# Transposed attention scores in exact widths and three banks per head, in a windowed-attention and SwiGLU-gate kernel

## The chip, the cores and the metric

One core of one Trainium2 chip. The metric is the device time of one execution in microseconds, the median over several runs. All inputs and outputs are float32 in HBM.

## The reference

```python
x = A_x                                   # 1 x 2048 x 512
xn = layernorm(x)
# A: attention, 32 heads of 16, query i sees keys i-255 .. i
q, k, v = split(xn @ wqkv)                # wqkv 512 x 1536
p = softmax(where(mask, q @ k.T * 16 ** -0.5, -1e9))
s = (p @ v) @ wo                          # wo 512 x 512
# B: SwiGLU, F = 1792
b = (silu(xn @ w_gate) * (xn @ w_up)) @ w_down
out = x + s * silu(b)
```

## The kernel before

**Stages.** The 2048 tokens go in four chunks of 512. For each chunk the kernel normalises and transposes x, projects q and k (`Proj`, tile a), v (`Values`, vp), the two halves of the SwiGLU (`GateUp`, g and u), its down projection (`Down`, d) and the output projection (`Wo`, s). All of these are "dense" matmuls of float32 values that are split into a high and a low part (format fp32r) and multiplied in three combinations. Their weights are fetched once per chunk (wr), split by ScalarE into wh (line 425) and by GpSimd into wl (line 428).

**Two streams on TensorE.** Each matmul uses 64 of the 128 rows of the array. Row group 0 does one half of each contraction, row group 1 the other, and both run side by side; `next_mm(r)` emits the next matmul of stream r. Short jobs of the attention are put in `extra[r]` and go first.

**Attention.** A unit u is one chunk and four heads; there are 32 units, 8 for each chunk. For each unit:

- b (`max_pair`, line 946): scores of 128 queries against up to 384 keys; VectorE takes the masked row maximum (line 954). The matmul is at least 256 columns wide: `w = max(n, 256)`.
- mt (`max_turn`, line 980): transposes the maxima, which are then put as an extra row into q by a small DMA, negated.
- c (`prob_pair`, line 1097): transposed scores, keys on the partitions and queries on the columns, minus the maximum. `pieces(c, e)` says which key blocks kb go into bank e of a head: each entry is (kb, first query block, columns of the matmul, place in the bank, first and last column that are used). ScalarE takes the exponential of the used columns (line 1058) and writes it into a round buffer p of `PCAP` columns (`p_place`, `p_take`); GpSimd sets the blocks on the two edges of the window to zero (`masks`, lines 1071 and 1075).
- pv (`pv_visit`, line 1134): the value product of the whole unit in plain fp32, 32 output columns for each head; after it the unit's part of p is free.

PSUM has 8 banks: four (`pf`) for the dense tiles and four (`pr`, `rb_free`) that b, c, mt, xp (the transposes of later chunks) and pv share.

**Order.** The program is written out by a planner while it is built: it keeps clocks of its own for TensorE's two streams (`issue(r, cols)`: `cols * 0.000444 + 0.004` us for a matmul) and for VectorE, ScalarE and GpSimd (`do(engine, ready, cost, ...)`), and issues what is due and ready by these clocks. `plan_attention` gives the due times: in `streams[1]` the score pairs of unit u from u + 1.07 on, its value product at u + 1.89, where 1 is the dense work of a unit (`PACE` = 17.6 us). Each engine then runs its instructions in this order.

Of the kernel before, what the change touches and what calls it, by code (L numbers as in the profile page):

```python
# [35 lines left out]
NEG = -1.0e30  # L36
QUART = ((0, 4), (4, 7), (7, 11), (11, 14))
NHID = 8
PCAP = 6784
NSL = 12  # L40
SPARE = 3
LAG = 7
# [13 lines left out]
def tile_window_attention_swiglu_gate(  # L56
# [305 lines left out]
    def half(r):  # L362
        return slice(R * r, R * r + R)
# [568 lines left out]
    def max_pair(u, p, qb):  # L932
        c = u // NG
        lo = qb * P
        n = 3 * P
        if c == 0 and qb < 2:
            lo, n = HALO, (qb + 1) * P
        w = max(n, 256)
        m = mts[u % 2]
        for h in range(2):  # L940
            j = 2 * p + h
            r = R * h
            pb, tag = bank(rb_free, f"b{u}_{qb}_{j}")

            def go(pb=pb, r=r):
                nc.tensor.matmul(  # L946
                    pb[:, :w], qs[u % 3][r : r + 48, p, qb * P : (qb + 1) * P],
                    ks[u % 3][r : r + 48, p, lo : lo + w], start=True, stop=True,
                )

            def ttr(pb=pb, j=j):
                junk = sb(f"jk{u}_{qb}_{j}", [P, 3 * P], BF16, "jk", 1)
                col = 8 * (j % 2) + 4 * (j // 2) + qb
                nc.vector.tensor_tensor_reduce(  # L954
                    junk[:, :n], pb[:, :n], maskb[:, 3 * P - n :], 1.0, -3.0e38,
                    ALU.add, ALU.max, m[:, col : col + 1],
                )

            def after(t, tag=tag):
                rb_free[tag] = t  # L960
                ttr_at[u] = ttr_at.get(u, []) + [t]

            extra[h].append((w, go, lambda t, ttr=ttr, after=after: do("V", t, 0.23 + 0.00098 * n, ttr, after, 0.0)))

    mtp = {}

# [40 lines left out]

    def pieces(c, e):
        if c == 0:
            return ([(3, 2, 256, 0, 128, 256), (2, 2, 256, 256, 256, 512)],  # L1010
                    [(0, 0, 384, 0, 0, 384)], [(1, 1, 384, 0, 0, 384)])[e]
        return ([(3, 2, 256, 0, 128, 256), (-2, 0, 256, 256, 256, 384)],
                [(-1, 0, 256, 0, 0, 256), (2, 2, 256, 256, 256, 512)],
                [(0, 0, 384, 0, 0, 384)], [(1, 1, 384, 0, 0, 384)])[e]

    pt = {}
    pt_at = {}
# [16 lines left out]
        p_next[0] = at + h * n  # L1034
        return pbuf[:, at : at + h * n].rearrange("p (h n) -> p h n", h=h)

    def prob_span(u, e):
        pcs = pieces(u // NG, e)
        return min(q[4] for q in pcs), max(q[5] for q in pcs)

    def prob_ready(u, e, p):
        a, b = prob_span(u, e)
        if p_place(2 * (b - a)) is None:
            return None
        return latest([ms_at.get(u), bank_time(rb_free, 2), p_freed[0]])

# [2 lines left out]
    def prob_pair(u, e, p):  # L1049
        c = u // NG  # L1050
        pcs = pieces(c, e)
        a, b = prob_span(u, e)
        t = p_take(2, b - a, u)
        pt[u, e, p] = t, a
        left = [2]

        def exp(h, pc):
            nc.scalar.activation(t[:, h, :], pc[:, a:b], AF.Exp, scale=DH ** -0.5)  # L1058

        blocks = []  # L1060
        for kb, qb, w, at0, v0, v1 in pcs:
            q0 = qb + (v0 - at0) // P
            for blk in range((v1 - v0) // P):
                if q0 + blk == kb or q0 + blk == kb + 2:
                    blocks.append((v0 + blk * P, q0 + blk == kb))

        def masks():
            for at, diagonal in blocks:
                s = t[:, :, at - a : at - a + P]
                if diagonal:  # L1070
                    nc.gpsimd.affine_select(  # L1071
                        s, s, [[0, 2], [1, P]], ALU.is_ge, 0.0, base=0, channel_multiplier=-1
                    )
                else:
                    nc.gpsimd.affine_select(  # L1075
                        s, s, [[0, 2], [-1, P]], ALU.is_gt, 0.0, base=0, channel_multiplier=1
                    )

        def after(tm, tag):
            rb_free[tag] = tm  # L1080
            left[0] -= 1
            if left[0] == 0:
                if blocks:
                    do("G", tm, 0.36 * len(blocks), masks, lambda t: pt_at.__setitem__((u, e, p), t), 0.0)
                else:
                    pt_at[u, e, p] = tm

        for h in range(2):
            r = R * h
            pc, tag = bank(rb_free, f"c{u}_{e}_{2 * p + h}")  # L1090

            def finished(t, h=h, pc=pc, tag=tag):
                do("S", t, 0.06 + 0.00081 * (b - a), lambda: exp(h, pc), lambda t: after(t, tag), 0.0)

            for i, (kb, qb, w, at0, _, _) in enumerate(pcs):
                def go(i=i, k0=HALO + kb * P, qb=qb, w=w, at0=at0, r=r, pc=pc):
                    nc.tensor.matmul(  # L1097
                        pc[:, at0 : at0 + w], ks[u % 3][r : r + 49, p, k0 : k0 + P],
                        qs[u % 3][r : r + 49, p, qb * P : qb * P + w],
                        start=(i == 0), stop=True, skip_group_check=True,  # L1100
                    )

                extra[h].append((w, go, finished if i == len(pcs) - 1 else None))
# [10 lines left out]
    def pv_visit(u, es):  # L1114
        c, g = divmod(u, NG)
        pbs = [bank(rb_free, f"pv{u}_{r}") for r in range(2)]
        jobs = [[], []]
        for e in es:
            for kb, qb, w, at0, v0, v1 in pieces(c, e):
                for r in range(2):  # L1120
                    k64 = 2 * kb + r
                    a, b = max(k64, 0), min(k64 + 5, 8)
                    jobs[r].append((b - a, e, kb, R * a, R * b, at0 + R * a - P * qb))
        for r in range(2):
            jobs[r].sort(key=lambda o: -o[0])
        begun = set()
        cost = 0.3
        for both in zip(*jobs):
            for r in range(2):
                n, e, kb, q0, q1, at = both[r]  # L1130
                assert vheld[(4 * c + kb) % VT, g // 4] == 4 * c + kb
                for j in range(4):
                    t, a = pt[u, e, j // 2]
                    nc.tensor.matmul(  # L1134
                        pbs[r][0][32 * j : 32 * j + 32, q0:q1],
                        vt[half(r), (4 * c + kb) % VT, VW * (4 * g + j) : VW * (4 * g + j) + 32],
                        t[half(r), j % 2, at - a : at - a + q1 - q0],
                        start=(r, j) not in begun, stop=True, skip_group_check=True,
                    )
# [41 lines left out]
    def plan_attention():  # L1181
        for u in range(NU):
            c = u // NG
            if u:
                marks.append((u - 1 + 0.3, load_qk, (u,)))
            for n in range(8):
                streams[0].append((u + 0.02 + 0.1 * n, max_ready, max_pair, (u, n // 4, n % 4)))
            streams[0].append((u + 0.8, turn_ready, max_turn, (u, 0)))
            streams[0].append((u + 0.8, turn_ready, max_turn, (u, 1)))
            ne = 3 if c == 0 else 4  # L1190
            for n in range(2 * ne):
                streams[1].append((u + 1.07 + 0.1 * n, prob_ready, prob_pair, (u, n // 2, n % 2)))
            streams[1].append((u + 1.89, pv_ready, pv_visit, (u, tuple(range(ne)))))
        for c in range(1, NCH):
            marks.append((8 * c - 4.9, load_x, (c,)))
# [261 lines left out]
```

## Time and profile before

| | |
|---|---|
| median of 3 runs | 871.28 us |
| lowest, highest | 868.6, 871.69 us |
| span of the profiled execution | 871.9 us |
| that execution's own time | not given beside its span |
| TensorE matmuls, weight loads | 864.0 us, 796.8 us busy, 11976 each |
| VectorE, ScalarE, GpSimd | 501.9, 486.7, 624.7 us busy |
| DMA | 139.63 MB |

How to read the profile: PE is TensorE's matmuls, PEld its weight loads, DVE VectorE, ACT ScalarE, POOL GpSimd, SP the engine that issues DMAs. A group's row gives the line of the kernel, the engine, the operation, output and inputs by the program's names, the shapes, the count, then busy us and the mean ns of one, and the idle time before them with what ended it. A matmul's record is longer than the time that it holds its stream, since matmuls are pipelined: the pace is read from start to start. In rows of the timeline the first two numbers are start and length in us. In rows of a window they are the window, its length, then busy us and count for PE, PEld, DVE, ACT and POOL, the granted share of TensorE's clock, the DMA share and GB/s. The launch parameters of the program are in the last lines of the kernel.

### The profile page before, as it was taken

Reading aid. Unit: us, or ns where it says so; the run is one execution under the profiler, and the core shown is the slowest. Engines: PE = TensorE matmul, PEld = TensorE weight load, DVE = VectorE, ACT = ScalarE, POOL = GpSimd, SP = SyncE. Lnnn points to the kernel's source line nnn. Section 1 sums busy time; section 2 is a strip of 40 time slices with the busy share of each in tenths; the row PEclk is TensorE's granted clock in tenths of the full one; section 3 lists DMA queues with packets and bytes.
Section 4 is the critical chain, followed back from the end, with each engine's and each line's share of the span. In section 5 each row is a group of like instructions: output and inputs, shape, how many; then the busy total and the mean of one; then the engine's idle time right before and its main releaser. Section 6 shows DMA issues by size and latency. Waiting matters only on the chain.

```text
span 871.9 us, 30169 instructions
## 1 busy us (share of the span) xinstructions
PE 864.0 (99%) x11976; PEld 796.8 (91%) x11976; DVE 501.9 (58%) x1663; ACT 486.7 (56%) x1040; POOL 624.7 (72%) x900
## 2 busy tenths in 40 slices
PE   9999999999999999999999999999999999999997
PEld 8799989898999998999999989999899989999897
DVE  4264476654765566666566676566655765554234
ACT  3345555555666465655576556665656665566431
POOL 4466587668777777867697797677768778869771
PEclk9999999999999999999999999999999999999999
DMA  5675846566686974766677877556667778654442
GB/s 138 157 182 126 235 115 173 125 161 166 149 200 181 261 190 103 145 159 133 151 181 193 220 178 200 120 147 144 169 141 187 160 194 208 163 132 112 104 124 79
DMA packets 69489, 139.63 MB, mean 160 GB/s; under 512 B 14546, under 2 KB 23250, under 8 KB 69348
## 3 DMA queue, kind: packets, MB, share of 16 engines
q1 hardware_dynamic: 69060, 137.18, 63.4%
q8 instruction: 94, 1.54, 0.8%
q10 hardware_dynamic: 288, 0.52, 0.2%
q14 instruction: 47, 0.39, 0.2%
HBM read 107.74 MB, written 29.62 MB: 158 GB/s over the span
## 4 chain that ended last, share of the span: by engine, by line
PE 96%; DMA 1%; DVE 1%; issue 1%; SPq 0%; ACT 0%; POOL 0%; DVEq 0%; ACTq 0%
PE u L457 19%; PE d L457 18%; PE g L457 17%; PE a L457 11%; PE pv L1134 8%; PE c L1097 5%; PE s L457 5%; PE b L946 5%; PE vp L457 5%; PE warm L234 1%; DMA den<-od 1%; DVE jk L954 0%; SPq L95 0%; PE xp L475 0%; POOL wl L428 0%
## 5 line engine op out<-in xcount | busy, mean ns | idle before, releaser
L428 POOL TENSOR_TENSOR wl<-wr,wh 128x512 fp32r<-128x512 f32 (+3 forms) x258 | 307.6, 1211 | 84.8 <-ACT wh L425 82.2
L954 DVE CUSTOM_DVE_ANT_0 jk<-b,maskb 128x384 bf16<-128x384 f32 (+2 forms) x512 | 271.3, 530 | 125.2 <-PE b L946 62.8
L1058 ACT ACTIVATE p<-c 128x384 f32<-128x384 f32 (+1 forms) x480 | 209.1, 489 | 129.6 <-PE c L1097 107.2
L457 PE MATMUL d<-wh,hh 64*128 64x256 f32 x1792 | 258.7, 278 | 0.3 <-DVE ho L454 0.3
L457 PEld LDWEIGHTS d<-wh,hh 64*128 64x128 f32 x1792 | 224.4, 185 | 1.5 <-issue 0.6
L457 PE MATMUL d<-wl,hh 64*128 64x256 f32 x896 | 203.5, 277 | 0.0
L425 ACT ACTIVATE wh<-wr 128x512 fp32r<-128x512 f32 (+3 forms) x258 | 142.1, 593 | 50.0 <-PE a L457 10.6
L457 PE MATMUL g<-xh,wh 64*128 64x512 f32 x448 | 169.0, 397 | 0.0
L457 PE MATMUL u<-xl,wh 64*128 64x512 f32 x448 | 168.3, 395 | 0.0
L457 PE MATMUL u<-xh,wh 64*128 64x512 f32 x448 | 168.3, 395 | 0.0
L457 PE MATMUL u<-xh,wl 64*128 64x512 f32 x448 | 167.9, 395 | 0.0
L457 PE MATMUL g<-xl,wh 64*128 64x512 f32 x448 | 167.0, 395 | 0.0
L457 PE MATMUL g<-xh,wl 64*128 64x512 f32 x448 | 166.7, 395 | 0.0
L1071 POOL TENSOR_SCALAR_AFFINE_SELECT p<-p 128x256 f32<-128x256 f32 x256 | 104.7, 414 | 78.8 <-ACT p L1058 75.6
L457 PEld LDWEIGHTS d<-wl,hh 64*128 64x128 f32 x896 | 147.6, 185 | 0.2
L946 PE MATMUL b<-k,q 48*128 48x384 f32 (+1 forms) x512 | 119.7, 335 | 0.5 <-DVE m L954 0.4
L1097 PE MATMUL c<-q,k 49*128 49x384 f32 (+1 forms) x704 | 115.3, 303 | 0.3 <-DVE m L954 0.3
L1075 POOL TENSOR_SCALAR_AFFINE_SELECT p<-p 128x256 f32<-128x256 f32 x224 | 92.5, 414 | 15.9 <-ACT p L1058 14.3
L457 PE MATMUL a<-xh,wh 64*128 64x512 f32 x256 | 99.1, 401 | 0.1
L457 PE MATMUL a<-xl,wh 64*128 64x512 f32 x256 | 98.5, 400 | 0.1
L601 POOL TENSOR_TENSOR hh<-h,hh 128x512 fp32r<-128x512 f32 x56 | 72.7, 1298 | 36.1 <-ACT hh L597 35.8
L457 PE MATMUL a<-xh,wl 64*128 64x512 f32 x256 | 98.3, 399 | 0.0
(114 smaller groups left out, 2096.7 us busy)
## 6 DMA issues: line engine op xcount, KB each, us to landing
wr<-wgu SPq DMA_DIRECT2D x112, 256.0 KB
k<-qkd SPq DMA_DIRECT2D x48, 192.0 KB
wr<-wqk SPq DMA_DIRECT2D x32, 256.0 KB
qkd<-qkh SPq DMA_DIRECT2D x32, 256.0 KB
qkd<-qkl SPq DMA_DIRECT2D x32, 256.0 KB
q<-qkd SPq DMA_DIRECT2D x64, 128.0 KB
wr<-wdn SPq DMA_DIRECT2D x32, 256.0 KB
od<-ev SPq DMA_DIRECT2D x32, 256.0 KB
```

The source lines that it names most:

```text
L234: nc.tensor.matmul(wbank[:, : rhs.shape[-1]], warm, rhs, start=True, stop=True)
L425: nc.scalar.activation(hi[0][pr, a:b], raw[pr, a:b], AF.Copy)
L428: nc.gpsimd.tensor_tensor(lo[0][pr, a:b], raw[pr, a:b], f32(hi[0][pr, a:b]), op=ALU.subtract)
L457: return nc.tensor.matmul(pb, a, b, start=first, stop=last, skip_group_check=True)
L601: nc.gpsimd.tensor_tensor(hl[:, 1, :], self.h, f32(hl[:, 0, :]), op=ALU.subtract)
L946: nc.tensor.matmul(pb[:, :w], qs[u % 3][r : r + 48, p, qb * P : (qb + 1) * P], ks[u % 3][r : r + 48, p, lo : lo + w], start=True, stop=True,)
L954: nc.vector.tensor_tensor_reduce(junk[:, :n], pb[:, :n], maskb[:, 3 * P - n :], 1.0, -3.0e38, ALU.add, ALU.max, m[:, col : col + 1],)
L1058: nc.scalar.activation(t[:, h, :], pc[:, a:b], AF.Exp, scale=DH ** -0.5)
L1071: nc.gpsimd.affine_select(s, s, [[0, 2], [1, P]], ALU.is_ge, 0.0, base=0, channel_multiplier=-1)
L1075: nc.gpsimd.affine_select(s, s, [[0, 2], [-1, P]], ALU.is_gt, 0.0, base=0, channel_multiplier=1)
L1097: nc.tensor.matmul(pc[:, at0 : at0 + w], ks[u % 3][r : r + 49, p, k0 : k0 + P], qs[u % 3][r : r + 49, p, qb * P : qb * P + w], start=(i == ...
L1134: nc.tensor.matmul(pbs[r][0][32 * j : 32 * j + 32, q0:q1], vt[half(r), (4 * c + kb) % VT, VW * (4 * g + j) : VW * (4 * g + j) + 32], t[hal ...
```

## The change

The matmuls of the scores get the width that is used: line 946 uses n columns, and `pieces` gives widths 128, 256 and 384 that fill three banks of 512 columns per head in chunks 1 to 3 (before: four banks with 256, 512, 384 and 384 used columns), and three banks with 512, 384 and 256 columns in chunk 0 (before 384 each). The exponential then covers a whole bank. The round buffer p grows from 6784 to 8192 columns, and a launch parameter sets the scratch for dynamic DMAs to 1024. The planner's price of an exponential and the due times of the score pairs are set anew.

```diff
-PCAP = 6784
+PCAP = 8192
...
-        w = max(n, 256)
...
-                    pb[:, :w], qs[u % 3][r : r + 48, p, qb * P : (qb + 1) * P],
-                    ks[u % 3][r : r + 48, p, lo : lo + w], start=True, stop=True,
+                    pb[:, :n], qs[u % 3][r : r + 48, p, qb * P : (qb + 1) * P],
+                    ks[u % 3][r : r + 48, p, lo : lo + n], start=True, stop=True,
...
-            extra[h].append((w, go, lambda t, ttr=ttr, after=after: do("V", t, 0.23 + 0.00098 * n, ttr, after, 0.0)))
+            extra[h].append((n, go, lambda t, ttr=ttr, after=after: do("V", t, 0.23 + 0.00098 * n, ttr, after, 0.0)))
...
     def pieces(c, e):
         if c == 0:
-            return ([(3, 2, 256, 0, 128, 256), (2, 2, 256, 256, 256, 512)],
-                    [(0, 0, 384, 0, 0, 384)], [(1, 1, 384, 0, 0, 384)])[e]
-        return ([(3, 2, 256, 0, 128, 256), (-2, 0, 256, 256, 256, 384)],
-                [(-1, 0, 256, 0, 0, 256), (2, 2, 256, 256, 256, 512)],
-                [(0, 0, 384, 0, 0, 384)], [(1, 1, 384, 0, 0, 384)])[e]
+            return ([(3, 3, 128, 0), (0, 0, 384, 128)], [(1, 1, 384, 0)], [(2, 2, 256, 0)])[e]
+        return ([(3, 3, 128, 0), (0, 0, 384, 128)], [(-2, 0, 128, 0), (1, 1, 384, 128)],
+                [(-1, 0, 256, 0), (2, 2, 256, 256)])[e]
...
-    def prob_span(u, e):
-        pcs = pieces(u // NG, e)
-        return min(q[4] for q in pcs), max(q[5] for q in pcs)
+    def prob_cols(u, e):
+        return sum(q[2] for q in pieces(u // NG, e))
...
-        if p_place(2 * (b - a)) is None:
+        if p_place(2 * prob_cols(u, e)) is None:
...
-            nc.scalar.activation(t[:, h, :], pc[:, a:b], AF.Exp, scale=DH ** -0.5)
+            nc.scalar.activation(t[:, h, :], pc[:, :n], AF.Exp, scale=DH ** -0.5)
...
-                do("S", t, 0.06 + 0.00081 * (b - a), lambda: exp(h, pc), lambda t: after(t, tag), 0.0)
+                do("S", t, 0.17 + 0.00084 * n, lambda: exp(h, pc), lambda t: after(t, tag), 0.0)
...
-            ne = 3 if c == 0 else 4
+            ne = 3
             for n in range(2 * ne):
-                streams[1].append((u + 1.07 + 0.1 * n, prob_ready, prob_pair, (u, n // 2, n % 2)))
+                streams[1].append((u + 1.07 + 0.13 * n, prob_ready, prob_pair, (u, n // 2, n % 2)))
...
-    nc = bacc.Bacc("TRN2", target_bir_lowering=False, num_devices=1)
+    nc = bacc.Bacc("TRN2", target_bir_lowering=False, num_devices=1, dynamic_dma_scratch_size=1024)
```

More of the change, by code (lines that the diff above doesn't have):

```diff
@@ L1035, in p_take @@
         return pbuf[:, at : at + h * n].rearrange("p (h n) -> p h n", h=h)
-    def prob_span(u, e):
-        pcs = pieces(u // NG, e)
-        return min(q[4] for q in pcs), max(q[5] for q in pcs)
+    def prob_cols(u, e):
+        return sum(q[2] for q in pieces(u // NG, e))
     def prob_ready(u, e, p):
-        a, b = prob_span(u, e)
-        if p_place(2 * (b - a)) is None:
+        if p_place(2 * prob_cols(u, e)) is None:
             return None
@@ L1051, in prob_pair @@
         pcs = pieces(c, e)
-        a, b = prob_span(u, e)
-        t = p_take(2, b - a, u)
-        pt[u, e, p] = t, a
+        n = prob_cols(u, e)
+        t = p_take(2, n, u)
+        pt[u, e, p] = t
         left = [2]
         def exp(h, pc):
-            nc.scalar.activation(t[:, h, :], pc[:, a:b], AF.Exp, scale=DH ** -0.5)
+            nc.scalar.activation(t[:, h, :], pc[:, :n], AF.Exp, scale=DH ** -0.5)
         blocks = []
[L1061 to L1065, printed above, removed]
+        for kb, qb, w, at0 in pcs:
+            for q in range(qb, qb + w // P):
+                if q == kb or q == kb + 2:
+                    blocks.append((at0 + (q - qb) * P, q == kb))
         def masks():
             for at, diagonal in blocks:
-                s = t[:, :, at - a : at - a + P]
+                s = t[:, :, at : at + P]
                 if diagonal:
@@ L1092, in finished @@
             def finished(t, h=h, pc=pc, tag=tag):
-                do("S", t, 0.06 + 0.00081 * (b - a), lambda: exp(h, pc), lambda t: after(t, tag), 0.0)
-            for i, (kb, qb, w, at0, _, _) in enumerate(pcs):
+                do("S", t, 0.17 + 0.00084 * n, lambda: exp(h, pc), lambda t: after(t, tag), 0.0)
+            for i, (kb, qb, w, at0) in enumerate(pcs):
                 def go(i=i, k0=HALO + kb * P, qb=qb, w=w, at0=at0, r=r, pc=pc):
@@ L1118, in pv_visit @@
         for e in es:
-            for kb, qb, w, at0, v0, v1 in pieces(c, e):
+            for kb, qb, w, at0 in pieces(c, e):
                 for r in range(2):
@@ L1132, in pv_visit @@
                 for j in range(4):
-                    t, a = pt[u, e, j // 2]
+                    t = pt[u, e, j // 2]
                     nc.tensor.matmul(
@@ L1136, in pv_visit @@
                         vt[half(r), (4 * c + kb) % VT, VW * (4 * g + j) : VW * (4 * g + j) + 32],
-                        t[half(r), j % 2, at - a : at - a + q1 - q0],
+                        t[half(r), j % 2, at : at + q1 - q0],
                         start=(r, j) not in begun, stop=True, skip_group_check=True,
```

## The prediction

> **What bounds the kernel now.** I read the page first, then the chain of waits, then the waits of the weight loads, then the groups by form, and last the order of time around single matmuls.
>
> ```profile
> span 871.9 us, 30169 instructions
> PE 864.0 (99%) x11976; PEld 796.8 (91%) x11976; DVE 501.9 (58%) x1663; ACT 486.7 (56%) x1040; POOL 624.7 (72%) x900
> ```
>
> TensorE has work in flight for 99% of the span; the other three have slack on average. The chain says the same by line:
>
> ```profile
> by line: PE u L457 19.0%; PE d L457 18.0%; PE g L457 17.2%; PE a L457 11.1%; PE pv L1134 8.3%; PE c L1097 5.5%; PE s L457 5.4%; PE b L946 4.7%; PE vp L457 4.7%; PE warm L234 1.3%; DMA den<-od 1.2%; issue 0.5%; DVE jk L954 0.5%; SPq L95 0.4%
> 836.24 15.43 PE d L457 x265
> ```
>
> The second line gives the pace. Two streams run side by side, one for each half of the array's rows; 265 matmuls of 256 columns take 15.43 us, so one takes 2 x 15.43 / 265 = 0.1165 us in its stream, 0.455 ns for a column. The scores c (L1097) hold 5.5%, 48.0 us, and their columns alone explain it: the rows below count 448 x 256 + 256 x 384 = 212,992 columns, half of them in each stream, and 106,496 x 0.455 ns = 48.5 us. So each score matmul costs its columns, and putting it between the dense ones costs next to nothing.
>
> ```profile
> L1097 PE MATMUL c<-q,k 49*128 49x256 f32 x448 | 57.9, 282 | 0.3 <-DVE m L954 0.3
> L1097 PE MATMUL c<-q,k 49*128 49x384 f32 x256 | 57.4, 340 | 0.0
> L946 PE MATMUL b<-k,q 48*128 48x256 f32 x64 | 13.3, 283 | 0.1
> L457 PE MATMUL g<-xh,wh 64*128 64x512 f32 x448 | 169.0, 397 | 0.0
> PEld pv L1134 <- issue: 4.9, 16, 0.4
> PEld pv L1134 <- POOL p L1075: 1.7, 5, 0.4
> PEld b L946 <- ACT p L1058: 0.4, 2, 0.2
> ```
>
> The last three are waits of the weight loads (total us, times, longest): these are small. Nothing but shorter PE streams can make this kernel much faster.
>
> **The change part by part.**
>
> *Narrower matmuls (the term that decides).* Per head, chunks 1 to 3 go from widths 256, 256, 256, 256, 384, 384 to 128, 384, 128, 384, 256, 256: two of 256 become 128. Chunk 0 goes from 256, 256, 384, 384 to 128, 384, 384, 256: one. Line 946 loses one for each head of chunk 0 (block 0). With 24 units of four heads and 8 of chunk 0 that is 192 + 32 + 32 = 256 matmuls, 128 in each stream. The count stays (704 and 512). By columns alone each would save 128 x 0.455 = 0.058 us, so 128 x 0.058 = 7.4 us at most.
>
> But a matmul needs its own weight load. Around 478 us a 64-column matmul (mt) sits in the stream of g, and shortly after one in that of vp:
>
> ```profile
> 478.19 0.40 PE L457 MATMUL g<-xl,wh 64*128 64x512 f32 x1
> 478.42 0.22 PE L980 MATMUL mt<-ident,m 64*80 64x64 f32 x1
> 478.45 0.47 PE L457 MATMUL g<-xh,wl 64*128 64x512 f32 x1
> 478.77 0.39 PE L457 MATMUL g<-xh,wh 64*128 64x512 f32 x1
> 478.76 0.27 PE L457 MATMUL vp<-wl,xh 64*128 64x256 f32 x1
> 478.89 0.25 PE L980 MATMUL mt<-ident,m 64*80 64x64 f32 x1
> 478.95 0.36 PE L457 MATMUL vp<-wh,xl 64*128 64x256 f32 x1
> 479.15 0.27 PE L457 MATMUL vp<-wh,xh 64*128 64x256 f32 x1
> 478.19 0.11 PEld L980 LDWEIGHTS mt<-ident,m 64*80 64x80 f32 x1
> 478.43 0.19 PEld L457 LDWEIGHTS g<-xh,wl 64*128 64x128 f32 x1
> 478.54 0.19 PEld L457 LDWEIGHTS g<-xh,wh 64*128 64x128 f32 x1
> ```
>
> From the g of 478.19 to that of 478.77 are 0.58 us, which hold two streams of 512 columns (2 x 0.233) and mt: mt took 0.114 us, about what 256 columns take, though it has 64. The loads say why: the load for the g behind mt begins at 478.43, when mt itself starts, and the next one only 0.11 later. The g that started at 478.45 shows 0.47 instead of 0.40: it stood waiting for its weights. In the vp stream mt cost 0.39 - 0.233 = 0.157, with a wait of its own in it. At the head of the kernel the loads stand alone:
>
> ```profile
> 10.65 0.28 PE L234 MATMUL warm<-rs,warm 128*128 128x4 f32 x2
> 10.55 0.30 PEld L234 LDWEIGHTS warm<-rs,warm 128*128 128x128 f32 x2
> 10.76 1.64 PEld L234 LDWEIGHTS warm<-warm 128*128 128x128 f32 x14
> 12.33 1.78 PEld L350 LDWEIGHTS xp<-ident,xt 128*128 128x128 f32 x16
> ```
>
> Two matmuls of 4 columns still take (10.76 - 10.55) / 2 = 0.105 us each, and sixteen of 128 columns (1.78 - 0.14) / 15 = 0.109. So a load of 128 columns has a pace of 0.105 to 0.114 us, and I take 0.109, the row with the width in question. A narrowed matmul then saves 0.1165 - 0.109 = 0.0075 us, 128 of them **1.0 us**. Bounds: at 0.105 it is 1.5 us; at full column pace 7.4 us; at 0.157 a loss of 128 x 0.04 = 5.2 us. The narrow shape itself does not occur in this trace in this number format.
>
> [...]
>
> *Exponentials.* Per head of chunks 1 to 3, before 256, 512, 384 and 384 columns, after three of 512; in chunk 0 384 three times becomes 512, 384, 256.
>
> ```profile
> L1058 ACT ACTIVATE p<-c 128x384 f32<-128x384 f32 x288 | 125.6, 490 | 63.7 <-PE c L1097 44.5 <-PE u L457 7.5 <-PE g L457 3.1
> L1058 ACT ACTIVATE p<-c 128x512 f32<-128x512 f32 x96 | 52.4, 597 | 25.0 <-PE c L1097 23.0 <-PE d L457 1.2 <-POOL wl L428 0.6
> L1058 ACT ACTIVATE p<-c 128x256 f32<-128x256 f32 x96 | 31.3, 381 | 40.9 <-PE c L1097 39.8 <-POOL p L1075 0.9
> L1071 POOL TENSOR_SCALAR_AFFINE_SELECT p<-p 128x256 f32<-128x256 f32 x256 | 104.7, 414 | 78.8 <-ACT p L1058 75.6 <-DMA q<-qkd 1.3 <-DMA k<-qkd 0.9
> L428 POOL TENSOR_TENSOR wl<-wr,wh 128x512 fp32r<-128x512 f32 x214 | 273.9, 1297 | 79.5 <-ACT wh L425 77.9 <-PE a L457 1.5
> ```
>
> That is 0.381 + 0.597 + 2 x 0.490 = 1.958 against 3 x 0.597 = 1.791 us, 0.167 less for each of 96 heads: ACT loses 16 us of 487. It idles 44% of the span and PE waits for it 0.4 us in all (the row above), so 0 is taken and 0.4 is the gain's end. A bank of scores is held longer by one exponential (0.597 instead of 0.490), but two pairs in eight fall away, so bank time falls.
>
> *Masks.* The blocks per unit stay at 8 for each pair of heads (6 in chunk 0). They come as 3, 3, 2 instead of 2, 2, 2, 2. What queues behind a batch on POOL is the split of weights (wl, 1.297 us each) and of hidden tiles, which dense matmuls need; a batch grows by one mask, 0.414 us. The last batch before the value product has two masks before and after, so its lateness stays. I take 0.
>
> *Buffer.* A unit fills 4 x 1536 = 6144 columns of p. Of 6784, 640 remain, room for one pair of 2 x 256 ahead of the value product; of 8192, 2048 remain, for two pairs of 2 x 512. The next unit's first pair is due 0.18 of a unit after that product, so room seldom decides; 0, with the 4.9 us of the row pv <- issue as an end for whatever is gained around the product.
>
> *The launch parameter* for DMA scratch.
>
> ```profile
> wr<-wgu SPq DMA_DIRECT2D x112, 256.0 KB
> ...
> xt<-x ACTq DMA_DIRECT2D x2, 256.0 KB
> ```
>
> These are the first of the 25 groups of DMA issues and the only one that is not SP's; POOL issues none, and no instruction names the parameter: 0. [...]
>
> *The planner.* It orders all instructions by a clock of its own. It will price a narrow matmul at 128 x 0.000444 + 0.004 = 0.061 us instead of the 0.109 I expect, so it believes PE earlier than it is; the other engines then have more time than planned, which does no harm. Its price of an exponential rises from 0.371 (for 384) to 0.600 (for 512), near the rows. The order of everything behind the first score shifts a little. Waits that a new order makes or removes I bound by the waits above, 3 us to either side.
>
> The sum: the median of the runs is 871.28 us, between 868.6 and 871.69; the page has only a span for its execution, 871.9, which is 0.6 above the median. Span 871.9 - 1.0 = 870.9; median 871.3 - 1.0 = **870.3 us**. Part of the runs' 3 us can be the clock at the start:
>
> ```profile
> 20.00:24.00 4.00, 4.00 (x21) 3.10 (x20) 0.15 (x1) 1.15 (x2) 0.63 (x2) 0.50 0.65 170
> L946 PE MATMUL b<-k,q x512: 275/337/443, 44.2 to 787.9; 48*128 48x384 f32 x149, 48*128 48x256 f32 x22
> ```
>
> For these 4 us TensorE had half its clock (0.50), which costs 2 us; the change touches nothing before the first score (b, 44.2 us), so this can fall either way.
>
> **The rivals.**
>
> *Columns count in full.* If the load for the matmul behind a narrow one ran further ahead, each would save 0.058 us: 871.3 - 7.4 = 863.8 us. For it: c's share of the chain matches its columns. Against: that is shown from 256 columns up, where the stream (0.1165) outlasts the load (0.109), and the load at 478.43 starts with mt, not before. [...]
>
> *Slower: a narrow matmul of this format runs like plain fp32.* For it: no matmul of this format under 256 columns is in the trace, so nothing there excludes it. A plain fp32 matmul of 128 columns is two instructions, seven calls in the row warm x14, each record (12.33 - 10.76) / 14 = 0.112, together 0.224 us: 0.108 more than now, 128 x 0.108 = 13.8 us, 885.1 us. It decides if it holds for any width under 256. Against: 282, 340 and 397 ns at 256, 384 and 512 columns lie on a line without a step, and each is one instruction.
>
> *Slower: the bunched masks arrive late.* If each of 24 value products waits for one mask more, 24 x 0.414 = 9.9 us, 881 us; half of that, 876. Against: the last batch does not grow, and five such waits make 1.7 us now.
>
> *A better order.* Fewer pairs and more room ahead of the value product, so that the 4.9 us of pv <- issue vanish with the 1.0: 865.4.
>
> **How the numbers follow.** Load pace 0.55; full columns 0.15; plain fp32 0.11; late masks 0.10; better order 0.09. A measurement of this kernel can tell about 0.5%, 4.4 us, from no change: 866.9 to 875.6. Faster: full columns, half of the better order (what is left of the waits decides) and 0.02 of the first case, 0.22. Slower: plain fp32, most of the late masks, and 0.07 of the first case where a narrow matmul costs as much as mt in the vp stream (871.3 + 5.2), 0.27. Same: 0.51. The range reaches from 863.6, the full columns, to 879, which takes in the 5.2 and most of the late masks; outside it are plain fp32 and the far end of the masks.
>
> **What would show it.** Right: c and b matmuls of 128 columns at about 282 - 58 = 224 ns long, one instruction each, the matmul behind one with a lengthened record as g had (0.47), and loads 0.11 apart; c's share of the chain near 5.4%; 384 exponentials; masks at 480. Wrong upward: two records for a narrow matmul, or one well over 280 ns. Wrong downward: c's share at 4.9% or less, and the matmul behind a narrow one at its usual length. Late masks would show as waits of pv for L1071 or L1075 in tens of times.

## The result and the profile after

The changed kernel takes 875.71 us (median of 6 runs, 873.07 to 878.75), the kernel before 871.12 (6 runs beside it): ratio 1.0055 [1.0033, 1.0077]. It is slower by about 4.6 us. Two further series gave 1.0024 [1.0005, 1.0044] and 1.0050 [1.0031, 1.0068]. The time lies inside the range on record, but the likeliest case was no change that can be told, and the small loss came from a step that had been priced at nothing, with 3 us to either side.

The profiled execution after is the slowest of its six: span 877.0 us, time 878.75. That of before has a span of 871.9, with 6.8 us of half clock at the start (17.7 to 24.6 us) that this one hasn't, which costs it 3.4 us. So the 5.1 us between the spans are not the loss itself.

The page:

```profile
span 877.0 us, 29908 instructions
PE 863.3 (98%) x11976; PEld 798.4 (91%) x11976; DVE 504.4 (58%) x1663; ACT 478.4 (55%) x944; POOL 623.1 (71%) x900
```

TensorE's count is as before, one record for each narrow matmul, ACT has 96 instructions fewer and is busy 8.3 us less. The groups by form (busy us, mean ns of one, idle before and what ended it):

```profile
L1053 ACT ACTIVATE p<-c 128x512 f32<-128x512 f32 x320 | 172.9, 596 | 109.7 <-PE c L1091 105.3 <-PE a L457 1.8 <-PE b L945 1.8
L1065 POOL TENSOR_SCALAR_AFFINE_SELECT p<-p 128x256 f32<-128x256 f32 x256 | 102.4, 413 | 66.6 <-ACT p L1053 59.9 <-DMA wr<-wdn 6.6
L1069 POOL TENSOR_SCALAR_AFFINE_SELECT p<-p 128x256 f32<-128x256 f32 x224 | 91.9, 413 | 22.0 <-ACT p L1053 20.8 <-DMA k<-qkd 0.9
L1091 PE MATMUL c<-q,k 49*128 49x384 f32 x256 | 65.0, 384 | 0.0
L1091 PE MATMUL c<-q,k 49*128 49x128 f32 x224 | 38.6, 226 | 3.0 <-DMA q<-ms 3.0
L1091 PE MATMUL c<-q,k 49*128 49x256 f32 x224 | 30.7, 280 | 0.0
L945 PE MATMUL b<-k,q 48*128 48x128 f32 x32 | 5.9, 229 | 0.7 <-DMA k<-qkd 0.7
```

The narrow matmul has one record of 226 ns (forecast about 224). 256 columns are as long as they were; 384 have 384 ns instead of 340, since many now stand behind a narrow one and wait for their weights (a place at 564 us below shows it; where the experiments widen the 128 again, they have 337 and 342 ns). Masks are 480, exponentials 384. New is the idle time in the fifth row: 3.0 us before the first c of two units, ended by the small DMA q<-ms that puts the maxima into q. The chain of waits (start, us, what) has that DMA twice among its ten longest pieces, at 98.68 and 243.68:

```profile
98.68 6.54 DMA q<-ms
243.68 6.71 DMA q<-ms
```

The timeline shows what it does, first SP's queue, then TensorE, then the windows (the number after POOL's is the granted clock):

```profile
97.22 1.36 SPq L95 DMA_DIRECT2D wr<-wgu  x1
98.68 0.60 SPq L95 DMA_DIRECT2D q<-ms  x1
```

```profile
105.35 0.55 PE L1091 MATMUL c<-q,k 49*128 49x128 f32 x4 [1.69 <-DMA q<-ms]
...
106.57 0.62 PE L457 MATMUL u<-xl,wh 64*128 64x512 f32 x1
```

```profile
20.00:24.00 4.00, 4.00 (x34) 3.19 (x34) 0.15 (x1) 0.28 (x1) 1.30 (x2) 1.00 0.90 221
104.00:106.00 2.00, 0.65 (x9) 0.68 (x11) 0.38 (x2) 0.09 (x1) 0.43 (x1) 1.00 1.09 360
106.00:108.00 2.00, 2.00 (x20) 2.00 (x18) 0.15 (x1) 1.16 (x3) 0.93 (x3) 0.55 1.02 227
108.00:110.00 2.00, 2.00 (x20) 2.00 (x18) 0.77 (x3) 0.92 (x2) 1.21 (x4) 0.59 1.02 173
```

The q<-ms of 8 KB is issued right behind a weight transfer and lands 6.5 us later; the planner takes it as landed 3.5 us after the transfers ahead of it. The c that needs it stands first in TensorE's queue and everything waits 1.69 us. Then the clock is granted at 0.55 and 0.59 for two windows, which loses 2 x 0.45 + 2 x 0.41 = 1.7 us more. In the first row the start runs at full clock.

How far the changed kernel is behind the kernel before, taken at the same dense matmul (the n-th of 7680) of both traces:

| place in the changed kernel (us) | behind (us) | what lies there |
|---|---|---|
| 16.0 | +1.5 | first dense matmul, after a longer wait at the head |
| 35.9 | -1.6 | full clock where before had half |
| 99.3 | -1.5 | |
| 118.5 | +1.8 | wait for q<-ms, then half clock |
| 245.2 | +2.2 | |
| 282.7 | +4.4 | wait of 1.34 for q<-ms at 250, then 0.85 by 283 in no single place |
| 311.5 | +5.4 | wait of 1.38 (issue) at 298 |
| 381.0 | +5.9 | |
| end | +5.1 | |

Behind 400 us the distance wanders, as the orders differ, but it no longer grows: its median is 4.5 to 5.8 us in each 100 us. So nothing is lost at every unit, as late masks or a dear narrow matmul would lose it; the loss sits at a few places.

### The profile page after: what moved, and what is told of

Same layout as the page of the kernel before. It is cut to its first block, busy times and chain, and to the rows that moved or that the text cites. A ratio compares the mean times of both kernels' runs of the same rounds, so it can differ in the third digit from the quotient of the medians.

```text
span 877.0 us, 29908 instructions
## 1 busy us (share of the span) xinstructions
PE 863.3 (98%) x11976; PEld 798.4 (91%) x11976; DVE 504.4 (58%) x1663; ACT 478.4 (55%) x944; POOL 623.1 (71%) x900
## 4 chain that ended last, share of the span: by engine, by line
PE 92%; DMA 4%; POOL 1%; DVE 1%; issue 1%; SPq 1%; ACT 1%; ACTq 0%; POOLq 0%; DVEq 0%
PE d L457 18%; PE u L457 18%; PE g L457 17%; PE a L457 10%; PE pv L1128 8%; PE c L1091 6%; PE s L457 5%; PE vp L457 5%; PE b L945 4%; DMA q<-ms 2%; PE warm L234 1%; DMA wr<-wgu 1%; POOL wl L428 1%; DMA k<-qkd 1%; SPq L95 1%
## 5 line engine op out<-in xcount | busy, mean ns | idle before, releaser
L1053 ACT ACTIVATE p<-c 128x512 f32<-128x512 f32 (+2 forms) x384 | 197.3, 569 | 129.7 <-PE c L1091 121.8
L457 PE MATMUL u<-xl,wh 64*128 64x512 f32 x448 | 164.4, 397 | 0.0
L457 PE MATMUL u<-xh,wh 64*128 64x512 f32 x448 | 164.1, 397 | 0.0
L457 PE MATMUL g<-xh,wh 64*128 64x512 f32 x448 | 163.8, 395 | 0.0
L457 PE MATMUL u<-xh,wl 64*128 64x512 f32 x448 | 163.1, 396 | 0.0
L945 PE MATMUL b<-k,q 48*128 48x384 f32 (+2 forms) x512 | 122.7, 331 | 2.2 <-DMA out<-y 0.8
L1091 PE MATMUL c<-q,k 49*128 49x128 f32 (+2 forms) x704 | 103.4, 300 | 3.0 <-DMA q<-ms 3.0
L457 PE MATMUL a<-xh,wh 64*128 64x512 f32 x256 | 94.3, 394 | 0.1
L457 PE MATMUL a<-xl,wh 64*128 64x512 f32 x256 | 94.0, 394 | 0.1
L1091 PEld LDWEIGHTS c<-q,k 49*128 49x128 f32 x704 | 84.4, 187 | 6.9 <-DVE m L953 2.3
```

Source lines behind the costliest of these rows:

```text
L457: return nc.tensor.matmul(pb, a, b, start=first, stop=last, skip_group_check=True)
L945: nc.tensor.matmul(pb[:, :n], qs[u % 3][r : r + 48, p, qb * P : (qb + 1) * P], ks[u % 3][r : r + 48, p, lo : lo + n], start=True, stop=True,)
L1053: nc.scalar.activation(t[:, h, :], pc[:, :n], AF.Exp, scale=DH ** -0.5)
L1091: nc.tensor.matmul(pc[:, at0 : at0 + w], ks[u % 3][r : r + 49, p, k0 : k0 + P], qs[u % 3][r : r + 49, p, qb * P : qb * P + w], start=(i == ...
```

## The experiments

Two readings stood against each other: the price of the new matmuls, or the order that the planner makes of the same work. Each series has its own runs of the kernel before on the same chip.

**What a narrow matmul costs.** First the changed kernel's order, with the 256 narrow matmuls issued with 256 columns again:

```diff
-                    pb[:, :n], qs[u % 3][r : r + 48, p, qb * P : (qb + 1) * P],
+                    pb[:, : max(n, 256)], qs[u % 3][r : r + 48, p, qb * P : (qb + 1) * P],
...
-            return ([(3, 3, 128, 0), (0, 0, 384, 128)], [(1, 1, 384, 0)], [(2, 2, 256, 0)])[e]
+            return ([(3, 3, 128, 384), (0, 0, 384, 0)], [(1, 1, 384, 0)], [(2, 2, 256, 0)])[e]
...
+                    if w == P:
+                        back = 1 if at0 else 0
+                        qb, w, at0 = qb - back, 2 * P, at0 - back * P
```

> The changed kernel with its order untouched, but all 256 matmuls of 128 columns issued with 256 columns again (the surplus lands in places that the next matmul of the bank overwrites). Theory A (a load of weights sets the pace, 0.110 us, so narrowing saved next to nothing and the loss comes from the new order): 0.6 to 1.5 us slower than the changed kernel, about 876.5. Rival B (columns count in full, and the new order lost some 12 us): 7 us slower, 883. Rival C (a narrow matmul costs more than a wide one, and that is the loss): 3 to 6 us faster, 870 to 873.

And the changed kernel unaltered, beside it:

> The changed kernel itself once more, on the same chip as the others: 875.7 us by every theory, within 2 us; the profile shows whether PE again waits for the small DMA q<-ms near 105 and 250 us (theory A: at least one of the two waits, 1 to 2 us each, since the order puts the first c of the unit 5 us behind that DMA).

Measured: 878.08 us, 1.0072 [1.0046, 1.0098], against 874.08, 1.0024 [1.0005, 1.0044] for the changed kernel. Widening costs 4.0 us [1.3, 6.7]: more than the 1 us that the load pace gives and less than the 7.4 of full columns. But the two profiles differ in waits too, so this pair doesn't give the size. The same pair was taken in an order without the wait (the next experiment's edit and the widening together):

> The kernel of e4 (changed kernel, q<-ms counted as landed 3 us later) with its order untouched, and the 256 narrow matmuls issued with 256 columns again. Here no wait for q<-ms stands in the way of the price. Theory A (load of weights sets the pace): 0.5 to 1.5 us slower than e4, 873.3; behind a narrow c the next matmul comes 0.110 to 0.114 us later in e4, behind a wide one 0.117 to 0.120 here. Rival B (columns count in full): 7 us slower, 879. Rival C (narrow costs more than wide): faster than e4, 869 to 871.

Measured: 873.7 us, 1.0034 [1.0015, 1.0053], where that order with narrow matmuls gave 1.0005 and 1.0017: 2 us, with an uncertainty of about 2. To multiply the cost instead, the 224 score matmuls of 256 columns were issued as two of 128:

```diff
+                    for x in range(0, w, P if w == 2 * P else w):
+                        y = P if w == 2 * P else w
...
-                        pc[:, at0 : at0 + w], ks[u % 3][r : r + 49, p, k0 : k0 + P],
-                        qs[u % 3][r : r + 49, p, qb * P : qb * P + w],
+                            pc[:, at0 + x : at0 + x + y], ks[u % 3][r : r + 49, p, k0 : k0 + P],
+                            qs[u % 3][r : r + 49, p, qb * P + x : qb * P + x + y],
```

> The kernel of e4 with its order untouched, and each of its 224 c matmuls of 256 columns issued as two of 128, with the same weights loaded for each. Columns stay the same, loads grow by 224, 112 in each stream. Theory A (a narrow matmul costs its load, 0.112 us): 112 x (2 x 0.112 - 0.119) = 11.8 us slower than e4, about 884. Rival B (columns count, loads are hidden): within 1 us of e4, 872 to 873.

> The kernel of e4 once more, as the base for e9 on the same chip: 0 to 2 us from the kernel before by every theory; no wait of PE for q<-ms.

Measured: 883.95 us, 1.0144 [1.013, 1.0158], against 872.31, 1.0017 [1.0002, 1.0033]: 11.6 us [10.9, 12.4]. If columns decided, two halves would cost what one whole does. 112 pairs in each stream take 11.64 / 112 = 0.104 us more than one matmul of 256 columns (0.1165), so one narrow matmul takes (0.1165 + 0.104) / 2 = 0.110 us. The groups of the split kernel, loads and matmuls of c:

```profile
L1093 PEld LDWEIGHTS c<-q,k 49*128 49x128 f32 x928 | 96.0, 186 | 3.9 <-DVE m L953 0.9
L1093 PE MATMUL c<-q,k 49*128 49x128 f32 x672 | 76.3, 248 | 0.6 <-DVE m L953 0.6
```

The 224 further loads are there and no wait of any size is new: the time goes into loads. One place in the unsplit kernel shows it singly, TensorE's matmuls and then its loads:

```profile
563.95 0.39 PE L457 MATMUL a<-xl,wh 64*128 64x512 f32 x1
...
564.18 0.22 PE L1091 MATMUL c<-q,k 49*128 49x128 f32 x1
...
564.24 0.40 PE L1091 MATMUL c<-q,k 49*128 49x384 f32 x2
564.47 0.39 PE L457 MATMUL a<-xh,wl 64*128 64x512 f32 x1
```

```profile
564.18 0.19 PEld L1091 LDWEIGHTS c<-q,k 49*128 49x128 f32 x2
564.29 0.19 PEld L457 LDWEIGHTS a<-xh,wl 64*128 64x128 f32 x1
```

Between the two a of one stream, 0.52 us apart, lie 512 columns of a (0.233) and a c of 128 and of 384 columns, which take 0.29 together. Taking 384 x 0.455 = 0.175 off leaves 0.115 for the narrow one. The load of the 384 columns begins as the narrow matmul starts, and that of the next a 0.11 later.

**The wait for q<-ms.** The planner takes the maxima as landed 3 us later than it did:

```diff
-            dma(t, put, lambda t: ms_at.__setitem__(u, t), -3.0, 8)
+            dma(t, put, lambda t: ms_at.__setitem__(u, t + 3.0), -3.0, 8)
```

In the changed kernel:

> The changed kernel with one planner constant more: the small DMA q<-ms counts as landed 3 us later, so the first scores c of a unit are ordered later. Theory A: PE's waits for q<-ms near 105 and 250 us go, 3 to 4 us, 872. Rivals C and D (loss by the narrow matmuls or by three banks): 875 to 876.

In the kernel before:

> The kernel before with the same margin of 3 us for q<-ms in the planner. Theory A (the loss is PE waiting for q<-ms, which the kernel before had only once, 0.4 us): as before, 870.5 to 873. Rival E (the margin helps any version by some 3 us, so e4 is only the changed kernel plus an unrelated gain): 868 to 870.

Measured: changed kernel 872.31, 1.0005 [0.9988, 1.0022], and 1.0017 in the repeat above; kernel before 874.73, 1.0037 [1.0022, 1.0052]. TensorE's waits of the changed kernel with this margin (us in total, times, longest) have no q<-ms left:

```profile
PE warm L234 <- DVE warm L229: 1.1, 1, 1.1
PE c L1091 <- DVE m L953: 0.6, 1, 0.6
```

Three series of the changed kernel average 1.0043 and two with the margin 1.0011, so the margin is worth about 2.8 us, with an uncertainty of about 1.4. The instructions are the same, so that much of the loss belongs to the order. But the same margin slows the kernel before, whose profile lists no wait of TensorE for q<-ms (two of the expectations name one of 0.4 us, which isn't in it). It shifts the order of everything, and that has a price apart from the wait. So the wait was then removed without touching the order of TensorE, VectorE, GpSimd or ScalarE's activations: the small DMA goes into ScalarE's queue.

```diff
-            move(qs[u % 3][48 : 113 : 64], box[0])
+            move(qs[u % 3][48 : 113 : 64], box[0], nc.scalar)
```

> The changed kernel with one edit: the small DMA q<-ms is issued from ACT's queue, not from SP's, where it stands behind transfers of weights. The order of PE, DVE, POOL and of ACT's activations stays exactly as it was. Theory A (PE waits for q<-ms, and the waits bring on stretches of half clock): waits for q<-ms near 105 and 250 us go, 2 to 4 us faster than e14, 871 to 873, and fewer runs with a clock of 0.997 or less. Rival I (the loss lies elsewhere in the order): within 1 us of e14.

> The changed kernel as the base for e13 on the same chip: 873 to 876 us by every theory, with waits of c for q<-ms in its profile.

> The kernel before with q<-ms on ACT's queue, its order unchanged. Theory A (it waited for q<-ms once, 0.4 us): within 1 us of the kernel before. Rival J (the queue helps any version, by shorter landings everywhere): 2 us or more faster, 868 to 869.

> The kernel of e4 (margin for q<-ms) with q<-ms on ACT's queue: by theory A there is no such wait left to remove, so as e4 and e10, 0 to 1.5 us above the kernel before. It is also the version here that might beat both: if the free place on SP's queue helps the weights, 869 to 870.

Measured, in this order: 874.11, 1.0036 [1.0021, 1.0052]; the changed kernel unaltered 874.45, 1.0050 [1.0031, 1.0068]; the kernel before with that queue 872.04, 1.0011 [0.9999, 1.0023]; margin and queue together 874.14, 1.0037 [1.0024, 1.0049]. TensorE's waits, unaltered and then with the other queue:

```profile
PE c L1091 <- DMA q<-ms: 1.9, 2, 1.4
```

```profile
PE s L457 <- issue: 2.0, 1, 2.0
...
PE c L1091 <- DMA q<-ms: 0.4, 1, 0.4
```

The wait falls from 1.9 to 0.4 us, the time only by 0.0014, 1.2 us (0.3 by the medians), with intervals that overlap: less than the 2 to 4 us of theory A, and close to the 1 us that rival I allows. Against it stands a price of the queue itself. In the kernel before it is 1.0 us, its interval just reaching nothing, and there a c now waits for q<-ms, which none did with SP's queue:

```profile
PE c L1097 <- DMA q<-ms: 1.0, 1, 1.0
```

In the order with the margin, which has no such wait to lose, the other queue costs 1.8 us [0.9, 2.7] (874.14 against 872.31 on the same chip), where nothing was forecast. And the changed kernel with it has a new wait of 2.0 us that ends at 293.7, for nothing that the profile shows. So this doesn't settle what the wait alone is worth.

**Orders of the same work.** The remaining edits change only prices or due times by which the planner sorts. The new price of an exponential, put into the kernel before, alone and with the margin:

```diff
-                do("S", t, 0.06 + 0.00081 * (b - a), lambda: exp(h, pc), lambda t: after(t, tag), 0.0)
+                do("S", t, 0.17 + 0.00084 * (b - a), lambda: exp(h, pc), lambda t: after(t, tag), 0.0)
```

> The kernel before, with nothing changed but the planner's price of an exponential (0.17 + 0.00084 n as in the change). Same instructions, another order. Theory A (orders differ by several us, and the change lost by its order): 2 us or more away from the kernel before, likelier slower, 873 to 877. Rival D (orders of the same work differ by less than 1 us, and the loss belongs to three banks and bigger exponentials): 870 to 872.

> The kernel of e3 (before, with the new price of an exponential) with the margin of 3 us for q<-ms. Theory A: e3's loss was the same wait, so it goes: 871 to 873, and no wait of c for q<-ms in the profile. Rival F (the price itself makes a worse order): 874 to 876, as e3.

Measured: 874.61, 1.0032 [1.0012, 1.0051], and 875.67, 1.0056 [1.0036, 1.0076]. A price closer to the rows makes the kernel before slower. With the margin the waits of c for q<-ms (1.6 us in five of them with the price alone) are gone, and the time doesn't fall, so theory A missed here: they were not what the new price cost. In the changed kernel a narrow matmul at its true price (in `issue`):

```diff
-        clock[r] = front[0] + cols * 0.000444 + 0.004
+        clock[r] = front[0] + max(cols, 240) * 0.000444 + 0.004
```

> The changed kernel, and the planner is told the true pace of a narrow matmul: issue() counts at least 240 columns (0.111 us). No margin for q<-ms. Theory A (the loss is the lead of the first c over q<-ms, which this does not set): waits for q<-ms remain, 873 to 877. Rival G (the loss comes from the planner's wrong price of narrow matmuls, 0.061 us): 870 to 872.

the old due step of the score pairs:

```diff
-                streams[1].append((u + 1.07 + 0.13 * n, prob_ready, prob_pair, (u, n // 2, n % 2)))
+                streams[1].append((u + 1.07 + 0.1 * n, prob_ready, prob_pair, (u, n // 2, n % 2)))
```

> The changed kernel with the old step of the due times (0.1 instead of 0.13), without margin for q<-ms: a further order of the same instructions. Theory A (orders of the same work lie 0 to 5 us apart, and the first c is still due right behind q<-ms): 872 to 877, with waits for q<-ms in the profile. Rival H (the wider step of the due times is what made the change slow): 870 to 871.

and the margin (the edit shown above) with the old price of an exponential:

```diff
-                do("S", t, 0.17 + 0.00084 * n, lambda: exp(h, pc), lambda t: after(t, tag), 0.0)
+                do("S", t, 0.06 + 0.00081 * n, lambda: exp(h, pc), lambda t: after(t, tag), 0.0)
```

> The changed kernel with the margin for q<-ms and the old, too low price of an exponential (0.06 + 0.00081 n). Theory A (order alone): anywhere from 870 to 876. Rival F (the higher price of an exponential makes the worse order): below e10, 869 to 871.

Measured: 875.84, 1.0056 [1.0038, 1.0075]; 873.16, 1.0028 [1.0014, 1.0042]; 876.23, 1.0059 [1.0041, 1.0077]. None of the three comes down to the 869 to 872 that its rival (G, H, F) forecast. The last has none of the waits for q<-ms and is still 3.9 us [2.5, 6.3] behind the order with the margin alone. It loses 3.9 us between 257 and 280 us. The windows of its trace (all matmuls in the first bracket), and two lines of its timeline:

```profile
266.00:270.00 4.00, 4.00 (x40) 3.54 (x40) 2.86 (x9) 2.24 (x5) 0.76 (x1) 1.00 0.92 192
270.00:274.00 4.00, 4.00 (x21) 3.17 (x20) 2.49 (x7) 3.08 (x6) 4.00 (x9) 1.00 0.55 203
```

```profile
270.75 0.40 PE L457 MATMUL a<-xh,wl 64*128 64x512 f32 x1
270.99 0.39 PE L457 MATMUL a<-xh,wh 64*128 64x512 f32 x1
...
274.25 0.39 PE L457 MATMUL a<-xh,wl 64*128 64x512 f32 x1
274.26 0.44 PE L945 MATMUL b<-k,q 48*128 48x384 f32 x1
```

PE is 100% busy in both windows, but the second holds 21 matmuls instead of 40. From 270.5 to 274.25 one a follows the other at 0.233 us and nothing runs beside them: one stream works, the other half of the array stands idle, and neither busy time nor the list of waits shows it. With the margin alone the same a run beside the matmuls of s. Why the planner holds the second stream here is not shown.

This can be added up. From the starts and lengths of all matmuls of a trace I laid each into the stream that it fits, took off its columns at 0.455 ns, and summed what is left between neighbours, halved for two streams, from 25 us on and without the value products. Gaps over 0.3 us are a stream that stands; those under 0.1 us I take for loads that are late, an estimate: where the width alone changes they differ by 5.2 and 6.3 us. Those in between (7 to 10 us) are in neither column. A half clock counts among them all.

| kernel | ratio | span of this profile | gaps over 0.3 us, sum | gaps under 0.1 us, sum |
|---|---|---|---|---|
| before | 1 | 871.9 | 11.9 | 8.4 |
| before, other queue | 1.0011 | 867.9 | 11.6 | 8.4 |
| before, margin | 1.0037 | 871.6 | 13.4 | 9.4 |
| before, price and margin | 1.0056 | 873.2 | 14.7 | 8.5 |
| before, price | 1.0032 | 875.7 | 17.4 | 8.1 |
| changed, margin (twice) | 1.0005, 1.0017 | 870.3, 869.3 | 12.9, 13.2 | 14.1, 14.1 |
| changed, old due step | 1.0028 | 870.7 | 15.4 | 13.4 |
| changed, margin and old price | 1.0059 | 874.5 | 16.3 | 13.8 |
| changed, margin and other queue | 1.0037 | 871.9 | 14.7 | 14.0 |
| changed, other queue | 1.0036 | 874.6 | 15.4 | 14.9 |
| changed (three times) | 1.0055, 1.0024, 1.0050 | 877.0, 871.7, 871.1 | 16.9, 14.5, 13.8 | 13.8, 13.8, 13.7 |
| changed, true price | 1.0056 | 879.6 | 21.4 | 14.1 |
| changed, wide again | 1.0072 | 880.0 | 18.8 | 8.6 |
| changed, margin, wide again | 1.0034 | 869.8 | 12.8 | 7.8 |

Spans of single executions follow the fourth column: with gaps of 11.6 to 13.2 us they lie at 868 to 870 us (before has the 3.4 us that the half clock at its start costs on top), with 13.4 to 15.4 at 871 to 875, from 16.3 up at 874 to 880. That is in part bookkeeping, as gaps are what a span holds beside columns; what it adds is that whole stretches of one stream make the difference, and not a little at each matmul. The last column is the narrow matmul: 5.4 us more small gaps with it (13.8 against 8.4; 5.2 and 6.3 in the two pairs that differ in width alone), against 7.4 us fewer columns. That leaves 1.1 to 2.2 us saved, as far as the small gaps hold the whole price.

So orders of the same instructions lie up to 0.6% apart. The kernel before is the fastest of its four (others 1.0032, 1.0037, 1.0056); the changed kernel, 1.0043 on average, is the third of its five (1.0005 to 1.0059). What is shown is that one and the same changed program takes 1.0011 in one order and 1.0059 in another, so the 0.4% is no more than order alone makes. The means of both families are alike, 1.0031 and 1.0039, but with four and five orders, which scatter by 0.002, a difference of 0.003 between them can't be excluded. That narrow widths and three banks are about neutral fits all of this; for the three banks with their bigger exponentials it is argued, as they were never run without the rest. No version here beat the kernel before.

## Why the prediction was wrong

**Narrow matmuls: right in mechanism and size.** A narrow matmul costs its load, 0.110 us by the split (0.115 at the place shown) against 0.109 in the forecast. The forecast took 1.0 us for the whole; the gaps say 1.1 to 2.2, the two widening pairs 2 and 4 with wide uncertainty. By the split's 0.110 it is 0.8. That the saving is small, between about 1 and 4 us, and isn't 7.4 is shown; where between is open. Full columns and the two instructions of plain fp32 are refuted by the split and by the single records.

**Exponentials, masks, buffer, launch parameter: nothing, as forecast.** ACT is busy 8 us less, not the 16 that the forecast worked out from the means of single records: these overlap (320 x 596 ns are 190.7 us, the row has 172.9 busy), and by the rows of the exponentials 12 us went (209.3 to 197.3). No gain came of it. Value products wait for masks hardly at all in the changed kernel (two of the weight loads' waits for pv; "issue" is a wait for nothing that the profile shows):

```profile
PEld pv L1128 <- issue: 6.2, 16, 1.3
...
PEld pv L1128 <- POOL rs L276: 0.4, 1, 0.4
```

No wait of pv for a mask reaches 0.3 us in that view, and the two rows of pv that name POOL at all make 0.7 us. The order with the margin has the same bunched masks, three such waits of 1.1 us in all, and takes 1.0005 and 1.0017. So late masks are refuted. What the launch parameter and the larger buffer do by themselves no run shows. The better order, which was to win 4.9 us at this place, didn't come either: 4.9 became 6.2.

**The planner: here the prediction failed.** It said that the new prices make TensorE look early, "which does no harm", and bounded waits of a new order by those of the old one, "3 us to either side". The bound is the step that failed: the waits of one order say nothing of what another order will make, and the order behind the new prices and due times lost 4.6 us where 3 were allowed and 0 were counted. The first statement isn't refuted: with the true price of a narrow matmul the kernel took 1.0056, no less than without it. In the order before no c waited for q<-ms; in the new one the c of two units came too early, 3.0 us in the first profile with 1.7 us of half clock behind, and one stream stood still for longer (gaps of 13.8 to 16.9 in three profiles, 11.9 before). No rival said that a re-sorted order alone could cost 0.5%, though the kernel's own description has every instruction placed by the planner's clocks.

**The start.** "Can fall either way" was right: the half clock is absent in this profile. But in the kernel before it is longer than the four us of the window in the forecast, and costs 3.4 us instead of 2, as the windows on both sides tell (6 x 0.19 + 4 x 0.50 + 6 x 0.05):

```profile
14.00:20.00 6.00, 5.78 (x23) 4.09 (x21) 2.43 (x5) 3.32 (x7) 4.97 (x4) 0.81 0.33 81
...
24.00:30.00 6.00, 6.00 (x52) 4.73 (x52) 1.50 (x4) 1.94 (x4) 2.02 (x3) 0.95 0.24 57
```

It is a reason to read spans of single executions with care, and not a reason for the loss.

**The signs that the prediction named.** 226 ns and one record (forecast 224), loads 0.11 apart, 384 exponentials, 480 masks: all as forecast. c's share of the chain is 6.0% where 5.4% was expected, likely because the chain also runs through the matmuls that wait behind narrow loads.

```profile
PE d L457 18%; PE u L457 18%; PE g L457 17%; PE a L457 10%; PE pv L1128 8%; PE c L1091 6%; PE s L457 5%; PE vp L457 5%; PE b L945 4%; DMA q<-ms 2%; PE warm L234 1%; DMA wr<-wgu 1%; POOL wl L428 1%; DMA k<-qkd 1%; SPq L95 1%
```

The line of the chain that is new is the 2% of the DMA q<-ms.

**What stays open.** What the wait for q<-ms costs by itself (between about 1 and 3 us), why TensorE's sequencer stands 1.3 to 2.2 us at the first s near 295 us in some of the orders, whether three banks and bigger exponentials cost or save anything by themselves, and why the planner's better prices give worse orders.

## What to carry to other kernels

Where a planner writes the order, any edit to a width or a price makes a new order, so price that as a term of its own: measure a few orders of the old kernel (a margin here, a price there) before a 0.5% difference is put down to the edit. Narrowing a matmul paid here only down to the time of its weight load, 0.110 us for 128 columns. With two streams on TensorE, a busy share of 100% didn't say that both ran (21 matmuls in one window of 4 us, 40 in the one before it): count matmuls in a window.

## What the runs showed of the hardware

A wait of TensorE can cost twice its length: behind that of 1.69 us in the changed kernel half clock lost 1.7 us more. Behind the first 28 us, and before the last spell at each kernel's end, all the profiles hold twelve idle spells of TensorE over 1.3 us. Five of them (1.69, 2.04, 2.10, 2.13 and 2.19 us) were followed by a stretch at half clock, and seven (1.32 to 1.52, and one of 1.80) were not. The stretch begins as work comes back or up to 1.2 us later. With the small DMA in ScalarE's queue, behind the wait of 2.04 us that ends at 293.7 (the number after POOL's is the clock):

```profile
293.00:295.00 2.00, 1.28 (x11) 1.28 (x12) 0.00 (x0) 0.00 (x0) 1.42 (x2) 0.69 0.93 256
295.00:297.00 2.00, 2.00 (x22) 2.00 (x22) 1.13 (x4) 0.60 (x1) 0.00 (x0) 0.50 0.77 267
```

In the kernel with the true price, behind a wait of 2.10 that ends at 105.40:

```profile
104.00:106.00 2.00, 0.60 (x4) 0.64 (x6) 0.26 (x2) 0.00 (x0) 0.29 (x1) 0.82 1.06 344
106.00:108.00 2.00, 2.00 (x17) 2.00 (x17) 0.15 (x1) 1.09 (x2) 0.54 (x2) 0.50 1.00 228
108.00:110.00 2.00, 2.00 (x25) 2.00 (x24) 0.33 (x1) 0.97 (x2) 0.58 (x2) 0.83 0.94 171
```

Here the loss is 2 x (0.18 + 0.50 + 0.17) = 1.7 us, as in the changed kernel, so such a stretch lasts 3.4 us. Of the six spells from 1.6 us up, five (1.7 to 2.2 us) were followed by one.

The records of the clock in the two traces of the main comparison give the lengths closer. In the kernel before, half clock runs from 17.73 to 24.56 us, 6.827 us, and full clock behind it for 846.505 us; in the changed kernel half clock runs from 106.21 to 109.63, 3.413 us, and full clock behind it for 764.585. In steps of 3.413 us these are 2, 248, 1 and 224. In each such step of these two traces, from the first with dense matmuls alone on, I added up the columns of both streams' matmuls at 0.455 ns, leaving out steps with value products. Half clock followed on five of 400 steps:

| kernel | step (us) | filled, of what two streams hold at full clock |
|---|---|---|
| before | 14.32 to 17.73 | 0.405 |
| before | 17.73 to 21.15 | 0.377 |
| before | 867.65 to 871.07 | 0, behind the last matmul |
| changed | 102.80 to 106.21 | 0.405 |
| changed | 870.80 to 874.21 | 0.192, with the last matmuls |

One more step came to 0.405, the last with matmuls in the kernel before (864.24 to 867.65), and full clock followed; the other 394 came to 0.50 or more, and full clock followed on all. What decides it is not shown beyond these steps.

For the other traces I counted such steps from where their windows put the half clock: 105.28 us with the true price, 293.76 with the other queue, and 105.76 and 300.32 in the changed kernel widened again, which is 57 steps apart. So counted, the five spells above lie each inside one step, but for 0.1 us of that of 2.10; that of 1.80 us, from 295.56 to 297.36 with the true price, is split by a step's end at 296.43. And one stream alone fills at most half: at the start of the kernel before, from 14.45 us on, it ran alone with 12 matmuls of 512 columns in the step that came to 0.405. The step at the start of the changed kernel, 17.47 to 20.88, came to 0.502, and full clock followed.

Half clock goes with the scatter of the runs: 9 of 30 executions of the changed kernel have a mean clock of 0.997 or less, 4 of 24 with the margin, and 6 of 118 of the kernel before.
